# The absolute value of E's phases on VectorE instead of ScalarE, one step ahead, in the last three batches of an S4D kernel

## The chip, the cores and the metric

One core of one Trainium2 chip runs the program alone. The metric is the device time of one execution in microseconds. The kernel before has a median of 719.2 us over three runs (718.16, 719.2 and 723.35). The profile shows one more execution of it, which took 723.32 us.

## What is computed

A block of two branches over 2048 tokens of 448 channels, both residual and behind a layer norm that is scaled and shifted by a modulation of a condition c. The first branch is an S4D state-space convolution, the second a mixer MLP over the tokens (W2 gelu(W1 LayerNorm(h)^T)):

```python
def _A_ref(u, log_A_real, A_imag, C_real, C_imag, log_dt, D_skip):
    L = u.shape[1]
    dt = jnp.exp(log_dt)
    A = -jnp.exp(log_A_real) + 1j * A_imag
    C = (C_real + 1j * C_imag) * dt[:, None]
    P = jnp.exp((A * dt[:, None])[:, :, None] * pos[None, None, :])
    K = 2.0 * jnp.einsum("dn,dnl->dl", C, P).real
    y = jnp.fft.irfft(Uf * Kf[None, :, :], L2)[:, :, :L]
    return y + u * D_skip[None, None, :]
...
h = _layernorm(x, axis=-1) * (1 + ca) + sa
x = x + ga * _A_ref(h, ...)
h = _layernorm(x, axis=-1) * (1 + cb) + sb
x = x + gb * _B_ref(h, ...)
```

Uf and Kf are the rfft of u and K. The part that matters here is K: for each of 448 channels, a sum over 256 states of a complex exponential over 2048 positions. The kernel splits a position into 64 x 32 and writes K as a product of two factors for each channel, E (over 64) and G (over 32), each a magnitude times the cosine and the sine of a phase.

## The kernel before

The channels are taken 16 at a time; a group of 16 has two halves of 128 states, and each half is one *step*: 56 steps, in 7 *batches* of 8. TensorE, ScalarE, VectorE and GpSimd take their instructions in the order in which the program is written; only the DMA queue on SyncE (SP) is ordered by the framework after the first steps.

A batch begins with a *window* (`window(s)`): for each of its 8 steps TensorE makes the exponents (`st_exponents`, L601) and ScalarE takes their Exp (L612) into `mag`. Then ScalarE loads the table of Sin and the 8 steps follow. In a step `s`:

- TensorE makes the phases of step s+1 (`st_phase`, L601): xe (for E) and xg (for G), each one PSUM bank, as four pairs of matmuls, xe and xg in turn. Each name has two buffers, so the phase of step s+1 takes the buffers of step s-1.
- From step 33 on TensorE then makes K of step s-1 (`st_kgen`, L676: 64 small matmuls of E and G into kg).
- ScalarE takes Abs of xe (L642, into `ab`) and of xg (L643), then the Sin of xe in place (L644), of xg (L645), of |xg| (L646) and of |xe| (L647). The last two are cosines: sin(pi/2 - 2 pi |x|). L647 writes into xg.
- GpSimd makes G (L649, L650), VectorE the two sine halves of E (L651, L652), then what `between()` holds, then the two cosine halves of E (L654, L655).
- Behind the step, ScalarE flushes its list: the copy of a finished kg (L690), copies of `vv` (L802), of `y` (L720).

From step 33 on, every second step also carries a *piece* of the convolution: TensorE multiplies a spectrum of K by a table (`pc_s2`, L770, into kx), VectorE multiplies it by the spectrum of u (L779, zx and zy, in the `between()` of the next step), GpSimd combines them (L781, L782, z), TensorE transforms back (`pc_inv`, L796, vv). In the window VectorE also copies `y` out of PSUM (L720). VectorE adds the skip to ks (L695) in the other steps' `between()`.

Behind the batches come the remaining pieces and then the MLP, which TensorE bounds.

Of the kernel before, what the change touches and what calls it, by code (L numbers as in the profile page):

```python
# [10 lines left out]

F32 = mybir.dt.float32
F32R = mybir.dt.float32r
BF16 = mybir.dt.bfloat16
AF = mybir.ActivationFunctionType
ALU = mybir.AluOpType
# [6 lines left out]
P = 128  # L23
# [7 lines left out]
BATCH = 8  # L31
# [129 lines left out]
class WeightStream:  # L161
# [12 lines left out]
    def load(self):  # L174
        n = self.loaded
        if n == 64:
            return
        w = self.pool.tile([P, 896], F32, tag="w", name="w", bufs=3)
        if n < 32:
# [14 lines left out]
    def begin(self, most):  # L194
# [4 lines left out]
        w = self.raw.pop(n)  # L199
        hi = self.pool.tile([P, 896], F32R, tag="whi", name="whi")  # L200
        lo = self.pool.tile([P, 896], F32R, tag="wlo", name="wlo")
        self.nc.scalar.copy(hi, w)  # L202
# [4 lines left out]
    def rest(self, part, eng, load=True):  # L207

        if part:
            w, hi, lo = part  # L210
            eng.tensor_tensor(lo, w, hi.bitcast(F32), ALU.subtract)  # L211
            if load:
# [4 lines left out]
def tile_adaln_s4d_mixer(ctx, tc, i, out):  # L217
# [4 lines left out]
    dram = ctx.enter_context(tc.tile_pool(name="dram", bufs=1, space=DRAM))  # L222
    pars = [dram.tile([2, 3, P, 2, N], F32, name=f"pars{q}") for q in range(4)]
    yu_d = dram.tile([2, 32, 2, 8, 4, D], F32, name="yu_d")
    us_d = dram.tile([2, 32, P, DC], F32, name="us_d")
    v_d = dram.tile([32, P, D], F32, name="v_d")
    x2_d = dram.tile([L, D], F32, name="x2_d")
# [10 lines left out]
    with ExitStack() as es:  # L238
        V, S, G, T = nc.vector, nc.scalar, nc.gpsimd, nc.tensor
        tt, ts, stt = V.tensor_tensor, V.tensor_scalar, V.scalar_tensor_tensor  # L240
# [9 lines left out]
        cg, mp, wp = right("cg", 1), right("mp", 8), right("wp", 2)  # L250
# [15 lines left out]
        def par_load(q):  # L266
            n = min(P, D - P * q)
            raws[q] = {}
            for nm in ("A_C_real", "A_C_imag", "A_log_A_real", "A_A_imag"):
                raws[q][nm] = qp.tile([P, N], F32, tag=nm, name=nm, bufs=2)  # L270
                nc.sync.dma_start(raws[q][nm][0:n], i[nm][P * q : P * q + n])
# [4 lines left out]
        par_load(0)  # L276
        tab = cg.tile([P, 3, 512], F32R, name="tab")
        for v in (2, 1, 0):
# [24 lines left out]

        lph = [cg.tile([P, N], F32R, name=f"lph{k}") for k in range(3)]
        lex = [cg.tile([P, N], F32R, name=f"lex{k}") for k in range(4)]
        for t in lex + lph:
# [56 lines left out]
        def chain(q):  # L363
# [8 lines left out]
            def split(src, places):  # L372
                hl = qp.tile([P, 2, N], F32R, tag="hl", name="hl", bufs=3)[0:n]
                V.tensor_copy(hl[:, 0], src)
                yield
                tt(hl[:, 1], src, hl[:, 0].bitcast(F32), ALU.subtract)
                for k, v in places:
                    nc.sync.dma_start(pars[q][v, k, 0:n], hl.bitcast(F32))
                yield
# [79 lines left out]
        def angle():  # L459

            for a, s, u, xa, ya in tmp.values():
                S.activation(xa, ya, AF.Arctan)
# [25 lines left out]
        nm = xp.tile([P, 16], F32, name="nm")  # L488
# [87 lines left out]
        mags, m2s, eg, phs = {}, {}, {}, {}  # L576
# [20 lines left out]
        def halves(out, lhs, rhs, start, stop):  # L597

            for k in range(2):
                r = slice(64 * k, 64 * k + 64)  # L600
                T.matmul(out[k], lhs[r], rhs[r], start=start, stop=stop)  # L601

        def st_exponents(s):
            g, h = divmod(s, 2)
            phs[s] = [pph.tile([P, 512], F32, tag=nm, name=nm) for nm in ("xe", "xg")]
            halves(phs[s], lex[g % 4][:, h * P : (h + 1) * P], tab[:, 2], True, True)
# [7 lines left out]
        def st_phase(s):  # L614

            g, h = divmod(s, 2)
            lhs = lph[g % 3][:, h * P : (h + 1) * P]
            pm = [pph.tile([P, 512], F32, tag=nm, name=nm) for nm in ("xe", "xg")]
            halves(pm, lhs, tab[:, 1], True, False)
            halves(pm, mg[:, 0], ones, False, False)  # L620
            halves(pm, mg[:, 1], ones, False, False)
            halves(pm, lhs, tab[:, 0], False, True)
            phs[s] = pm

        def st_mag2(s):
# [4 lines left out]
            G.tensor_tensor(m2, me, w[:, :, None].to_broadcast([P, GD, 32]), ALU.mult)  # L630
            m2s[s] = m2

        def st_step(s, between):
            me, mg_, m2 = v32(mags[s][:, 0]), v32(mags[s][:, 1]), m2s.pop(s)
            E = gp_.tile([P, 2, GD, NJ], F32, tag="E", name="E")
            Gt = gp_.tile([P, 2, GD, NI], F32, tag="G", name="G")


            xe, xg = phs.pop(s)
            ab, sg, cg_ = (wp.tile([P, 512], F32, tag=nm, name=nm, bufs=b) for nm, b in (("ab", 1), ("gs", 3), ("gs", 3)))  # L640

            S.activation(ab, xe, AF.Abs)  # L642
            S.activation(cg_, xg, AF.Abs)  # L643
            S.activation(xe, xe, AF.Sin, scale=TWO_PI)  # L644
            S.activation(sg, xg, AF.Sin, scale=-TWO_PI)  # L645
            S.activation(cg_, cg_, AF.Sin, scale=-TWO_PI, bias=math.pi / 2)  # L646
            S.activation(xg, ab, AF.Sin, scale=-TWO_PI, bias=math.pi / 2)  # L647
            se, ce = v32(xe), v32(xg)
            G.tensor_tensor(Gt[:, 1], mg_, v32(sg), ALU.mult)  # L649
            G.tensor_tensor(Gt[:, 0], mg_, v32(cg_), ALU.mult)  # L650
            V.tensor_tensor(E[:, 1, :, 32:64], m2, se, ALU.mult)  # L651
            V.scalar_tensor_tensor(E[:, 1, :, 31::-1], me[:, :, 31::-1], -1.0, se, ALU.mult, ALU.mult)  # L652
            between()
            V.tensor_tensor(E[:, 0, :, 31::-1], me[:, :, 31::-1], ce, ALU.mult)  # L654
            V.tensor_tensor(E[:, 0, :, 32:64], m2, ce, ALU.mult)  # L655
            eg[s] = (E, Gt)
            mags.pop(s)
# [5 lines left out]
        def mellow():  # L663
            ready.extend(fresh)
            fresh.clear()
# [302 lines left out]
        def window(s):  # L968
            angle()
            logs(s == 8)  # L970
            if s == 8:
                u_scale()
                u_norm(0)
                u_norm(1)

            if s in (8, 16):
                for k in (0,) if s == 8 else (4, 5):
                    modulation(k, 0, 1)
            if s == 0:
                st_exponents(s)  # L980
            for e in range(BATCH):
                st_exp(s + e)

                if e + 1 < BATCH:
                    st_exponents(s + e + 1)
                else:
                    st_phase(s)
                mellow()
                if s == 8 and e == 0:
                    tt(mod[1], mod[1], mod[2], ALU.mult)  # L990
                flush(dve)
                flush(act)
                if s < 32:
                    more(WPACE[s // 8][e])
                if s == 0 and e >= 4:
                    u_stats(e - 4)
                if s == 8 and e == 1:

                    tt(mod[0], mod[0], mod[2], ALU.mult)
                if s and e < (2 if s <= 32 else 1):  # L1000
                    st_kgen(s - (2 if s <= 32 else 1) + e)
                elif e == 5:
                    if s == 8:
                        yks[0] = y0.tile([P, 32, DC], F32, tag="yk", name="yk0")
                    st_s1(s > 16)

                if s in (8, 16):
                    some(u_rows, rows, (2, 2, 2, 2, 2, 0, 1, 1)[e])
                elif s == 24 and e != 5:
                    some(u_cols, cols, 1)  # L1010

                if s >= 40 and e == 2:
                    piece(False)
                if s >= 32 and e in (4, 7):
                    piece(e == 4 and pieces[0] < NP, V)
                if s == 0 and e in (4, 5):
                    st_mag2(e - 4)
                elif s and (e < 2 or s >= 32):
                    st_mag2(s + e)
                if s == 8 and e == 0:  # L1020
                    u_norm(e + 2)
                if s == 0 and e == 3:
                    for r in range(4):
                        dsk_copy(r)
            if s == 0:

                S.activation(one, one, AF.Sin)
# [6 lines left out]
        for s in range(tail):  # L1034
            if s == 32:
                early.close()
                fp = es.enter_context(tc.tile_pool(name="fp", bufs=2, reuse_waits="tile"))
# [20 lines left out]
            def between():  # L1058
                flush(dve)
                if 2 <= s < BATCH:  # L1060
                    for r in range(2 * s, 2 * s + 2):
                        u_stats(r)
                if s < len(pace):
                    more(pace[s])
# [110 lines left out]
    with ExitStack() as es:  # L1175
        es.enter_context(tc.manual_schedule(engines={ENG.PE, ENG.Activation, ENG.DVE, ENG.Pool}))
        V, S, G = nc.vector, nc.scalar, nc.gpsimd
# [184 lines left out]
```

## Time and profile before

| | us |
|---|---|
| median of three runs | 719.2 |
| the profiled execution | 723.32 |
| its span, first to last instruction | 721.5 |
| steps 32 to 55 with their windows, from the table load of Exp at 245.41 to the start of the last L655 at 375.52 | 130.1 |
| ScalarE busy over the span | 442.9 |
| VectorE busy over the span | 453.3 |
| TensorE busy over the span | 630.4 |

A row of a timeline has the start in us from the span's start, the duration, the engine, the line, the operation, what it writes and reads, and, in brackets, how long the engine was idle before it and what ended that. Instructions of one engine overlap a little at their ends, so that the time one takes from its engine is read from start to start. A row of the windows view has the stretch and its length, then the busy time of each engine, the granted clock of TensorE, the share of the DMA engines and their rate.

### The profile page before, as it was taken

To read this page: it belongs to the slowest core of one execution; us is meant where nothing else is said; L and a number is where in the kernel's file an instruction comes from. 1 tells how busy PE (TensorE), PEld (TensorE's weight loads), DVE (VectorE), ACT (ScalarE), POOL (GpSimd) and SP (SyncE) were. 2 spreads that over 40 slices of the span, in tenths; PEclk is the share of its full clock that TensorE was granted. 3 is DMA by queue.
4 is the path that set the end of the run, shared out by engine and by line. 5 is a ranking of instruction groups with operands and counts; after the bars stand their busy time and mean duration, and the time that the engine had idled before them with its cause. 6 is when DMAs were issued, how large, how long until landed. Compare 5 with 4: busy or idle time off the path is not lost. (4 is left out here: it accounts for less than half of the span.)

```text
span 721.5 us, 18291 instructions
## 1 busy us (share of the span) xinstructions
PE 630.4 (87%) x7204; PEld 455.2 (63%) x7204; DVE 453.3 (63%) x875; ACT 442.9 (61%) x879; POOL 273.4 (38%) x328
## 2 busy tenths in 40 slices
PE   0659989987899888789888949999999999999997
PEld 0334334543544546556565617778999999999996
DVE  7569779769859768476785538778723263334441
ACT  5837588777988889989983549787622242222220
POOL 6487428318729788878884600000000000000000
PEclk9869857787999999989999959999999999999999
DMA  7795464356889645535236979974585436655540
GB/s 168 203 192 139 147 198 138 114 186 164 245 250 254 183 137 131 162 86 152 71 105 184 289 221 257 243 207 112 167 233 153 143 106 176 175 156 153 154 141 25
DMA packets 101636, 121.19 MB, mean 168 GB/s; under 512 B 13067, under 2 KB 87423, under 8 KB 101423
## 3 DMA queue, kind: packets, MB, share of 16 engines
q1 hardware_dynamic: 100014, 113.16, 55.3%
q0 software_dynamic: 1536, 6.87, 4.4%
q8 instruction: 57, 0.93, 0.6%
q14 instruction: 29, 0.23, 0.1%
HBM read 84.64 MB, written 34.87 MB: 166 GB/s over the span
## 5 line engine op out<-in xcount | busy, mean ns | idle before, releaser
L202 ACT CAST whi<-w 128x896 fp32r<-128x896 f32 x64 | 59.7, 938 | 131.4 <-PE o L1329 84.6
L649 POOL TENSOR_TENSOR G<-mag,gs 128x512 f32<-128x512 f32 x56 | 71.9, 1283 | 92.4 <-ACT gs L645 92.4
L211 DVE TENSOR_TENSOR wlo<-w,whi 128x896 fp32r<-128x896 f32 x64 | 68.0, 1087 | 40.3 <-ACT whi L202 27.9
L601 PE MATMUL xg<-tab,lph 64*128 64x512 f32 x112 | 68.0, 609 | 26.6 <-issue 7.9
L1194 PE MATMUL acc<-h3h,whi 128*128 128x448 f32 x224 | 83.5, 373 | 0.1
L1195 PE MATMUL acc<-h3l,whi 128*128 128x448 f32 x224 | 82.0, 366 | 0.0
L1329 PE MATMUL o<-ul,whi 128*128 128x448 f32 x224 | 81.3, 363 | 0.0
L676 PEld LDWEIGHTS kg<-E,G 128*32 128x32 f32 x3584 | 60.7, 121 | 32.5 <-issue 19.4
L1328 PE MATMUL o<-uh,whi 128*128 128x448 f32 x224 | 81.2, 362 | 0.0
L1196 PE MATMUL acc<-h3h,wlo 128*128 128x448 f32 x224 | 81.1, 362 | 0.0
L1330 PE MATMUL o<-uh,wlo 128*128 128x448 f32 x224 | 80.6, 360 | 0.0
L601 PE MATMUL xe<-tab,lph 64*128 64x512 f32 x112 | 66.7, 599 | 12.2 <-ACT gs L646 10.0
L676 PE MATMUL kg<-E,G 128*32 128x64 f32 x3584 | 70.8, 237 | 3.1 <-issue 2.3
L650 POOL TENSOR_TENSOR G<-mag,gs 128x512 f32<-128x512 f32 x56 | 71.7, 1280 | 0.0
L651 DVE TENSOR_TENSOR E<-m,xe 128x512 f32<-128x512 f32 x56 | 38.2, 683 | 39.6 <-ACT xe L644 31.5
L630 POOL TENSOR_TENSOR m<-mag,w 128x512 f32<-128x512 f32 x56 | 59.9, 1069 | 6.0 <-DVE E L655 1.5
L1332 DVE SCALAR_TENSOR_TENSOR y<-o,b,mod 128x448 f32<-128x448 f32 x16 | 10.9, 684 | 80.3 <-PE o L1330 80.3
L642 ACT ACTIVATE ab<-xe 128x512 f32<-128x512 f32 x56 | 33.6, 600 | 31.0 <-PE xe L601 18.4
L1194 PEld LDWEIGHTS acc<-h3h,whi 128*128 128x128 f32 x224 | 42.4, 189 | 13.9 <-ACT h L1250 6.3
L601 PE MATMUL xe<-tab,lex 64*128 64x512 f32 x56 | 31.2, 567 | 19.2 <-DMA lex<-wm 17.4
L601 PEld LDWEIGHTS xg<-tab,lph 64*128 64x128 f32 x112 | 24.0, 214 | 37.1 <-issue 9.8
L612 ACT ACTIVATE mag<-xe 128x512 f32<-128x512 f32 x56 | 35.5, 634 | 17.8 <-PE xg L601 11.1
(231 smaller groups left out, 1485.9 us busy)
## 6 DMA issues: line engine op xcount, KB each, us to landing
w<-in_B_w_dram SPq DMA_DIRECT2D x64, 224.0 KB
w<-in_B_w_dram SPq DMA_DIRECT2D x32, 448.0 KB
yu_d<-yt SPq DMA_DIRECT2D x16, 448.0 KB
yi<-yu_d SPq DMA_DIRECT2D x32, 224.0 KB
us_d<-uo SPq DMA_DIRECT2D x16, 448.0 KB
u<-us_d SPq DMA_DIRECT2D x32, 224.0 KB
v_d<-vt SPq DMA_DIRECT2D x32, 224.0 KB
vt<-v_d SPq DMA_DIRECT2D x16, 448.0 KB
```

What stands on the lines that cost most here:

```text
L211: eng.tensor_tensor(lo, w, hi.bitcast(F32), ALU.subtract)
L601: T.matmul(out[k], lhs[r], rhs[r], start=start, stop=stop)
L630: G.tensor_tensor(m2, me, w[:, :, None].to_broadcast([P, GD, 32]), ALU.mult)
L649: G.tensor_tensor(Gt[:, 1], mg_, v32(sg), ALU.mult)
L650: G.tensor_tensor(Gt[:, 0], mg_, v32(cg_), ALU.mult)
L676: T.matmul(kgs[g][32 * q : 32 * q + 32, m], Gt[:, c, d], E[:, c, d], start=h == 0 and c == 0 and m == 0, stop=h == 1 and c == 1, skip_grou ...
L1194: nc.tensor.matmul(acc[f], hi[:, fs], h3h[:, r], start=r == 0, stop=False)
L1195: nc.tensor.matmul(acc[f], hi[:, fs], h3l[:, r], start=False, stop=False)
L1196: nc.tensor.matmul(acc[f], lo[:, fs], h3h[:, r], start=False, stop=r == 15)
L1328: nc.tensor.matmul(o, hi[:, ks], uh[kh][:, k], start=kh == 0 and k == 0, stop=False)
L1329: nc.tensor.matmul(o, hi[:, ks], ul[kh][:, k], start=False, stop=False)
L1330: nc.tensor.matmul(o, lo[:, ks], uh[kh][:, k], start=False, stop=kh == 1 and k == 6)
```

## The change

From step 32 on ScalarE no longer makes `ab`. VectorE makes it by clearing the sign bit of xe, read out of PSUM as integers: of step s+1 in step s, behind the two sine products and ahead of `between()` and the two cosine products; of a batch's first step at the end of its window, behind the copies of y. Two buffers of `ab` take turns, one in each of two pools. The steps before 32 are unchanged.

```diff
+        abss = {}
+
+        def st_abs(s, xe):
+            abss[s] = (wp if s < 32 or s % 2 else fp).tile([P, 512], F32, tag="ab", name="ab", bufs=1)
+            if s < 32:
+                S.activation(abss[s], xe, AF.Abs)
+            else:
+                ts(abss[s].bitcast(I32), xe.bitcast(I32), 0x7FFFFFFF, None, ALU.bitwise_and)
+
...
-            ab, sg, cg_ = (wp.tile([P, 512], F32, tag=nm, name=nm, bufs=b) for nm, b in (("ab", 1), ("gs", 3), ("gs", 3)))
-
-            S.activation(ab, xe, AF.Abs)
+            sg, cg_ = (wp.tile([P, 512], F32, tag="gs", name="gs", bufs=3) for _ in range(2))
+
+            if s < 32:
+                st_abs(s, xe)
+            ab = abss.pop(s)
             S.activation(cg_, xg, AF.Abs)
             S.activation(xe, xe, AF.Sin, scale=TWO_PI)
...
             V.scalar_tensor_tensor(E[:, 1, :, 31::-1], me[:, :, 31::-1], -1.0, se, ALU.mult, ALU.mult)
+            if s >= 32 and (s + 1) % BATCH:
+                st_abs(s + 1, phs[s + 1][0])
             between()
...
                     st_phase(s)
+                    if s >= 32:
+                        st_abs(s, phs[s][0])
                 mellow()
```

On VectorE, step 46 (its E is E_5018) and its place before; xe_4896 is the xe of step 46, xe_4975 that of step 47:

```order
L651 TENSOR_TENSOR E_5018<-m2_4542,xe_4896 128x16x32
L652 SCALAR_TENSOR_TENSOR E_5018<-mag_4531,xe_4896 128x16x32
L779 TENSOR_TENSOR zx_5033<-kx_4961,u_4465 128x448
L779 TENSOR_TENSOR zy_5034<-kx_4961,u_4465 128x448
L654 TENSOR_TENSOR E_5018<-mag_4531,xg_4897 128x16x32
L655 TENSOR_TENSOR E_5018<-m2_4542,xg_4897 128x16x32
```

The same step on VectorE now (its E is E_5020, its xe is xe_4898, that of step 47 xe_4977; 14 to 16 lines further down in the file):

```order
L663 TENSOR_TENSOR E_5020<-m2_4542,xe_4898 128x16x32
L664 SCALAR_TENSOR_TENSOR E_5020<-mag_4531,xe_4898 128x16x32
L641 TENSOR_SCALAR ab_5033<-xe_4977 128x512
L793 TENSOR_TENSOR zx_5035<-kx_4963,u_4465 128x448
L793 TENSOR_TENSOR zy_5036<-kx_4963,u_4465 128x448
L668 TENSOR_TENSOR E_5020<-mag_4531,xg_4899 128x16x32
L669 TENSOR_TENSOR E_5020<-m2_4542,xg_4899 128x16x32
```

One instruction has come in, which reads the xe of the next step, and four of this step stand behind it.

On ScalarE, the first step of the batch that begins with step 48, before, with the engines each instruction waits for:

```order
L642 ACTIVATE ab_5376<-xe_5344 128x512 [waits PE_49,Activation_49]
L643 ACTIVATE gs_5378<-xg_5345 128x512 [waits PE_49]
L644 ACT_TABLE_LOAD
L644 ACTIVATE xe_5344<-xe_5344 128x512 [waits Activation_49]
L645 ACTIVATE gs_5377<-xg_5345 128x512
```

The same place on ScalarE now:

```order
L613 ACTIVATE mag_5341<-xg_5332 128x512 [waits PE_49]
L655 ACTIVATE gs_5379<-xg_5345 128x512 [waits PE_49]
L656 ACT_TABLE_LOAD [waits DVE_49]
L656 ACTIVATE xe_5344<-xe_5344 128x512 [waits Activation_49]
L657 ACTIVATE gs_5378<-xg_5345 128x512
```

The Abs is gone, and the table load ahead of the Sin that overwrites xe now waits for VectorE. On VectorE the and of this step stands directly behind the two copies of y:

```order
L734 COPY yk1_3527<-y1_5290 128x32x2x8
L734 COPY yk1_3527<-y1_5291 128x32x2x8
L641 TENSOR_SCALAR ab_5354<-xe_5344 128x512
L663 TENSOR_TENSOR E_5376<-m2_5208,xe_5344 128x16x32
L664 SCALAR_TENSOR_TENSOR E_5376<-mag_5156,xe_5344 128x16x32
```

Before, L651 of this step followed the copies; the and is new there too.

More of the change, by code (lines that the diff above doesn't have):

```diff
@@ L12 @@
 F32 = mybir.dt.float32
+I32 = mybir.dt.int32
 F32R = mybir.dt.float32r
```

## The prediction

> **What bounds the kernel now.** I read the stretch that the change touches, steps 32 to 55, first by its busy times, then engine by engine. Steady steps of the middle batch (40 to 47), as the windows view has them:
>
> ```profile
> core 0: us, PE busy (x) PEld busy (x) DVE busy (x) ACT busy (x) POOL busy (x), PEclk, DMA share, GB/s
> 317.00:333.00 16.00, 13.81 (x382) 9.70 (x380) 14.36 (x26) 15.20 (x33) 13.83 (x14) 1.00 0.45 132
> ```
>
> ScalarE (ACT) is busy 15.20 of 16 us, but VectorE (DVE), TensorE (PE) and GpSimd (POOL) are all near 14. Whoever takes work off ACT has about one microsecond in ten to give. ACT's timeline, from the copy of kg at the end of step 44 to the Sin of step 47:
>
> ```profile
> 321.26 0.37 ACT L690 COPY ks<-kg 128x256 f32<-128x256 f32 x1 [0.32 <-PE kg L676]
> 321.53 0.60 ACT L642 ACTIVATE ab<-xe 128x512 f32<-128x512 f32 x1
> 322.02 0.60 ACT L643 ACTIVATE gs<-xg 128x512 f32<-128x512 f32 x1
> 322.50 0.62 ACT L644 ACTIVATE xe<-xe 128x512 f32<-128x512 f32 x1
> ...
> 329.93 0.62 ACT L644 ACTIVATE xe<-xe 128x512 f32<-128x512 f32 x1
> ```
>
> Instructions overlap at their ends, so I count from start to start: the removed activation is worth 0.49 us (321.53 to 322.02), not its 0.60. Two steps, Sin to Sin, take 7.43 us (322.50 to 329.93). VectorE over the same two steps:
>
> ```profile
> 321.87 0.68 DVE L655 TENSOR_TENSOR E<-m,xg 128x512 f32<-128x512 f32 x1
> 323.22 0.69 DVE L651 TENSOR_TENSOR E<-m,xe 128x512 f32<-128x512 f32 x1 [0.68 <-ACT xe L644]
> 323.82 0.68 DVE L652 SCALAR_TENSOR_TENSOR E<-mag,xe 128x512 f32<-128x512 f32 x1
> 324.42 0.59 DVE L695 TENSOR_TENSOR ks<-ks,dsk 128x4 f32<-128x4 f32 x1
> 324.94 0.67 DVE L654 TENSOR_TENSOR E<-mag,xg 128x512 f32<-128x512 f32 x1
> 325.53 0.68 DVE L655 TENSOR_TENSOR E<-m,xg 128x512 f32<-128x512 f32 x1
> 326.33 0.69 DVE L651 TENSOR_TENSOR E<-m,xe 128x512 f32<-128x512 f32 x1
> 326.93 0.68 DVE L652 SCALAR_TENSOR_TENSOR E<-mag,xe 128x512 f32<-128x512 f32 x1
> 327.53 0.62 DVE L779 TENSOR_TENSOR zx<-kx,u 128x448 f32<-128x448 f32 x1
> 328.07 0.61 DVE L779 TENSOR_TENSOR zy<-kx,u 128x448 f32<-128x448 f32 x1
> 328.60 0.67 DVE L654 TENSOR_TENSOR E<-mag,xg 128x512 f32<-128x512 f32 x1
> 329.19 0.68 DVE L655 TENSOR_TENSOR E<-m,xg 128x512 f32<-128x512 f32 x1
> ```
>
> From L655 of step 44 (321.87) to L655 of step 46 (329.19) is 7.32 us. Without the waits ahead of the two L651, and with 0.60 for each L655 in front of them (as L651 to L652), the slots sum to 0.60+0.60+0.60+0.52+0.59+0.60+0.60+0.60+0.54+0.53+0.59 = 6.37 us. VectorE has 0.95 us free in two steps. In the same stretch TensorE runs, in its own order:
>
> ```profile
> 322.65 0.46 PE L601 MATMUL xg<-tab,lph 64*128 64x512 f32 x1 [1.02 <-ACT gs L643]
> 323.72 1.10 PE L676 MATMUL kg<-E,G 128*32 128x64 f32 x64
> 324.75 0.98 PE L770 MATMUL kx<-yk,si 128*64 128x224 f32 x8
> 325.66 1.03 PE L796 MATMUL vv<-z,si 64*128 64x224 f32 x8
> 326.36 0.56 PE L601 MATMUL xe<-tab,lph 64*128 64x512 f32 x1
> 327.02 0.58 PE L601 MATMUL xe<-tab,lph 64*128 64x512 f32 x1
> ```
>
> The first row is the phase of step 46. Its xg takes the buffer of step 44, so it cannot start before L655 of step 44 has read it: 0.78 us from 321.87 to 322.65 (the row names L643, but L655 ended at 322.55 too). The last two rows are the phase of step 47, which comes behind kgen (L676), L770 and L796; its xe is ready at 327.02 + 0.58 = 327.60.
>
> The delay of a batch reaches the end of the program, since the chain of waits leaves the batches through the last piece without slack:
>
> ```profile
> 379.89 0.08 DVE ks L695
> ...
> 380.06 0.67 POOL z L781
> ...
> 380.77 1.32 PE vv L796 x8
> ```
>
> **What is taken away.** ACT loses 24 activations of 0.49 us, 11.8 us. In each steady pair ACT would need 7.43 - 0.98 = 6.45 us. So another limit comes next.
>
> **What is added on VectorE.** 24 bitwise ands, 128x512, out of PSUM. The nearest row is the copy out of PSUM of the same size; the other two are the slowest and a quick tensor_scalar of half the size, from SBUF:
>
> ```profile
> L720 DVE COPY yk<-y 128x512 f32<-128x512 f32 x14 | 8.9, 678 | 0.9 <-PE y L714 0.9
> L388 DVE TENSOR_SCALAR s<-s 128x256 f32<-128x256 f32 x2 | 1.6, 800 | 0.0
> L423 DVE TENSOR_SCALAR u<-u 128x256 f32<-128x256 f32 x2 | 0.6, 294 | 0.1
> ```
>
> I take 0.60 us from start to start, what L651 to L652 takes at the same 0.68 duration. The ends, from the half sizes, are 2 x 0.29 = 0.59 and 2 x 0.80 = 1.6. Two ands make 1.20 in a pair where 0.95 is free: VectorE alone would need 6.37 + 1.20 = 7.57 us.
>
> **What is moved.** On SP, in several places of these steps, the load of a piece's u now stands behind two loads of lph instead of ahead of them. Each u is loaded three pieces before its zx, each lph two groups before its phase, so I cost this at nothing; without that cover it would be one issue on SP. The order on PE and POOL is as it was.
>
> **The new wait.** The and of step 47 stands in step 46 behind L652 and ahead of zx, zy, L654 and L655. It needs the xe of step 47, and VectorE takes instructions in order. So L654 and L655 of step 46 now wait for TensorE, and L655 is what lets the next phase start. That closes a round through rows above: L655 of step 44 to its released phase 0.78; to kgen 1.07 (322.65 to 323.72); to L770 1.03; to L796 0.91; to the phase of step 47 0.70; to its xe 1.24; a signal 0.06 (estimate); the and 0.60; zx 0.54; zy 0.53; L654 0.59; L655 again. The sum is 8.05 us, against 7.32 before in this round and 7.43 Sin to Sin. Before, only ACT read the xe that was ready at 327.60, and its Sin of it came at 329.93. Behind the waiting and are queued zx and zy (POOL's z waits for them) and the two cosine products (kgen and the next phase wait). A batch has two such rounds (steps 43 to 45 and 45 to 47): +0.73 at VectorE's 7.32, +0.62 at 7.43, together +1.35.
>
> **The start of a batch.** The Sin overwrites xe in place, so the table load ahead of it now waits for the and, which stands behind VectorE's two yk copies. Batch 48:
>
> ```profile
> 343.31 1.27 DVE L720 COPY yk<-y 128x512 f32<-128x512 f32 x2
> ...
> 344.25 0.62 ACT L643 ACTIVATE gs<-xg 128x512 f32<-128x512 f32 x1
> 344.89 1.28 ACT L644 ACT_TABLE_LOAD   x1
> ```
>
> The copies end at 344.58, the and at about 345.2: the load starts 0.3 us later instead of 0.5 earlier. With another and, 0.6, ahead of L654 of the batch's first step, L655 there is about 0.7 later (0.3 + 0.6, less what L654 waited for its cosine, an estimate), and the phase two steps on waits for it; two steps on, ACT waits for kgen:
>
> ```profile
> 305.81 0.76 PE L601 MATMUL xg<-tab,lph 64*128 64x512 f32 x1 [0.98 <-DVE E L655]
> 313.94 0.37 ACT L690 COPY ks<-kg 128x256 f32<-128x256 f32 x1 [2.92 <-PE kg L676]
> ```
>
> Against these 0.7 stands the 0.5 saved behind that copy, and a phase that ran at half clock and would run a little later, at the full one. I take 0, bounds -0.5 and +0.7.
>
> **Sum.** 3 batches x 1.35 = +4.0 us; with the bounds of the start +2.5 to +6.1. The profiled execution took 723.32 us (span 721.5), so it would take 727.3. It is the slow end of the three runs (718.16 to 723.35); on the median of 719.2 the same 4.0 gives **723.2 us**, +0.6%, below the 1% (7.2 us) that a measurement here can tell from no change.
>
> **Rivals.**
>
> *The clock falls within the steps (slower).* TensorE's longest gap in a round is 1.02 now; with rounds of 8 us and no more work it grows to about 1.7 (1.02 + 0.73). The granted clock moves in steps of 3.4 us:
>
> ```profile
> 243.84:247.26 3.42, 2.39 (x68) 1.57 (x68) 3.42 (x7) 3.39 (x7) 2.52 (x2) 0.99 0.39 93
> 247.26:250.67 3.41, 3.41 (x103) 2.80 (x106) 0.72 (x2) 2.23 (x6) 2.58 (x5) 0.51 0.76 228
> ...
> 257.50:260.91 3.41, 1.95 (x17) 1.18 (x16) 1.30 (x3) 3.38 (x6) 2.10 (x4) 1.00 0.35 111
> 260.91:264.32 3.41, 1.59 (x12) 0.79 (x16) 2.48 (x5) 3.41 (x9) 2.45 (x2) 0.99 0.57 179
> ```
>
> It fell to 0.51 behind a stretch with 2.39 us busy, and held behind one with 1.95. A round would leave some 1.7 busy in its emptiest stretch, so either can happen. It decides where a fall meets the 5.0 us of TensorE's links in the round (1.07+1.03+0.91+0.70+1.24): half clock for 3.4 us adds up to 1.7. One fall in each of six rounds is +10.2: 733.4 us. Chance 0.20.
>
> The Trainium skill ("TensorE: Matmul & The Clock Gate", Part 1) says that the clock is halved after an idle window of about 3.4 us and restored after a busy one. By that rule a gap of 1.7 us would cost nothing and the sum would stay 723.2; the trace agrees on the window's length, but its 2.39 us busy ahead of a fall speak against so clean a condition, so I keep the chance.
>
> *VectorE alone bounds.* If the xe is there in time, the rounds take 7.57: +0.25 and +0.14, three times, +1.2: 720.4 us. For it: the wait in my sum is only 0.48 a round. Against: the six rows of TensorE stand in that order whatever VectorE does. Chance 0.21.
>
> *ACT's time is simply won.* 11.8 us off: 707.4. It needs an and below 0.47 us and no wait in VectorE's queue; the L720 row speaks against it. Chance 0.05.
>
> *The and is dear.* At 1.6 us a round grows by another 1.0 and the start of a batch by 1.0: about +4.4 a batch, +13, 732.2 us. For it only the L388 row, which reads SBUF. Chance 0.06.
>
> **How the numbers follow.** My case has 0.48. Its own range is 2.5 to 6.1 on the median, 721.7 to 725.3, and the runs lie 1.0 below to 4.2 above their median. The range 717.5 to 731.0 takes in this, the second rival with that spread, and a clock that falls in about half of the rounds; it leaves out the rest of the clock's, the won ACT and the dear and, some 0.2. Faster by over 1%: only the won ACT, 0.05. Slower by over 1% (above 726.4): most of the clock's 0.20 and the dear 0.06, 0.23. Within: 0.72.
>
> **What would show it.** The and's row near 0.68 us; VectorE waiting for PE's xe ahead of the and in steps 44 and 46; Sin to Sin of 8.0 in the pairs 43 to 45 and 45 to 47; ACT waiting for kg longer than 0.3 to 0.4; the table load of Sin waiting for VectorE. The prediction is wrong if the pairs come out below 7.4, if the and takes half or twice 0.68, or if the clock's row shows 0.5 in steps 43 to 47.

## The result, and the profile after

The changed kernel took **730.2 us** (median of 4 runs, 729.43 to 730.55) against 719.65 (4 runs, 718.16 to 723.35): the ratio is 1.013, 95% interval 1.0097 to 1.0163, so slower, though by less than 2%. On another chip, beside the last experiments, it was 730.63 against 718.74, ratio 1.0179 (1.0155 to 1.0203). The time lies in the predicted range, near its upper end; the likeliest case, 723.2, was 7 us too low.

The profiled execution took 730.55 us. The page's span and the first line of its busy times:

```profile
span 728.8 us, 18271 instructions
PE 631.8 (87%) x7204; PEld 457.2 (63%) x7204; DVE 467.4 (64%) x899; ACT 431.9 (59%) x855; POOL 273.0 (37%) x328
```

ScalarE lost 11.0 us (442.9 before), VectorE gained 14.1, and the span grew by 7.3. The and itself, in the view that groups steps 32 to 55 by line, and what VectorE waited for ahead of it:

```profile
L641 DVE TENSOR_SCALAR ab<-xe 128x512 int32<-128x512 int32 x24 | 16.5, 686 | 10.5 <-PE xg L602 6.2 <-PE xe L602 4.2
L709 DVE TENSOR_TENSOR ks<-ks,dsk 128x4 f32<-128x4 f32 x11 | 7.4, 674 | 4.1 <-ACT ks L704 4.1
```

The and takes 686 ns, and VectorE stood 10.5 us ahead of it until TensorE had made an xe or xg. (Both halves of a phase are made together, so the name of either stands for it.) The second row, the add of the skip to ks, averaged 548 ns over the same eleven adds before; it will matter.

Of these 10.5 us, 4.6 stand in the three rounds in which the clock will be seen to fall, and 5.8 in the first steps of the batches. In the other three rounds the wait is hardly there. VectorE in step 54, one of them:

```profile
378.82 0.67 DVE L664 SCALAR_TENSOR_TENSOR E<-mag,xe 128x512 f32<-128x512 f32 x1
379.53 0.69 DVE L641 TENSOR_SCALAR ab<-xe 128x512 int32<-128x512 int32 x1
```

From start to start this is 0.71 us where 0.60 is the length without a wait; the others are 0.59 to 0.70. What filled the time is told with the experiments.

The Sin of step s to that of step s+2 is one pair. In batch 48, ScalarE's Sin of steps 51, 53 and 55:

```profile
363.73 0.60 ACT L656 ACTIVATE xe<-xe 128x512 f32<-128x512 f32 x1
...
373.31 0.60 ACT L656 ACTIVATE xe<-xe 128x512 f32<-128x512 f32 x1
...
381.44 0.60 ACT L656 ACTIVATE xe<-xe 128x512 f32<-128x512 f32 x1
```

9.58 and 8.13 us. All pairs, read in this way from both profiles (us; the second, fourth, sixth and eighth step of each batch):

| pair of steps | before, batches 32, 40, 48 | after |
|---|---|---|
| 2nd to 4th | 8.16, 9.43, 8.11 | 8.50, 9.59, 8.45 |
| 4th to 6th | 7.33, 7.32, 7.33 | 9.59, 8.19, 9.58 |
| 6th to 8th | 7.43, 7.43, 7.43 | 8.14, 9.44, 8.13 |

Of the six rounds of which the prediction spoke (the last two lines), three take 8.13 to 8.19 and three 9.44 to 9.59. The windows view of the changed kernel, cut at the steps of the clock, shows what the three long ones share:

```profile
core 0: us, PE busy (x) PEld busy (x) DVE busy (x) ACT busy (x) POOL busy (x), PEclk, DMA share, GB/s
270.72:274.13 3.41, 1.79 (x30) 0.96 (x34) 3.41 (x10) 3.03 (x7) 2.60 (x4) 1.00 0.38 103
274.13:277.55 3.42, 3.42 (x67) 2.33 (x58) 3.42 (x6) 2.54 (x5) 2.95 (x3) 0.50 0.65 11
325.33:328.75 3.42, 1.96 (x40) 1.12 (x44) 3.42 (x7) 3.17 (x7) 2.69 (x4) 1.00 0.58 180
328.75:332.16 3.41, 3.41 (x60) 2.29 (x50) 3.41 (x6) 2.31 (x5) 3.12 (x3) 0.50 0.04 14
362.88:366.29 3.41, 1.79 (x31) 0.96 (x30) 3.41 (x7) 2.98 (x7) 2.49 (x4) 1.00 0.25 68
366.29:369.71 3.42, 3.42 (x70) 2.32 (x61) 3.42 (x6) 2.51 (x5) 3.11 (x4) 0.50 0.02 5
```

In each batch, a stretch in which TensorE is busy 1.79 to 1.96 of 3.41 us is followed by one at half clock, in which it is busy throughout. Before, no round held such a stretch.

The ledger of steps 32 to 55 (table load of Exp to the start of the last cosine product): 130.1 before, 245.04 to 384.45 = 139.4 after, +9.3. The three undisturbed rounds give the price of a round at full clock: 4th to 6th 8.19 - 7.33 = +0.86, 6th to 8th 8.135 - 7.43 = +0.70, together +1.56 a batch, +4.7. The clock adds 1.40, 1.39 and 1.30, +4.1. The pairs 2nd to 4th add 0.84, and the part ahead of them gives back 0.3.

### The profile page after: what moved, and what is told of

Same layout as the page of the kernel before. It is cut to its first block, busy times and chain, and to the rows that moved or that the text cites. A ratio compares the mean times of both kernels' runs of the same rounds, so it can differ in the third digit from the quotient of the medians.

```text
span 728.8 us, 18271 instructions
## 1 busy us (share of the span) xinstructions
PE 631.8 (87%) x7204; PEld 457.2 (63%) x7204; DVE 467.4 (64%) x899; ACT 431.9 (59%) x855; POOL 273.0 (37%) x328
## 5 line engine op out<-in xcount | busy, mean ns | idle before, releaser
L690 PE MATMUL kg<-E,G 128*32 128x64 f32 x3584 | 72.3, 240 | 2.8 <-issue 1.3
L1344 PEld LDWEIGHTS o<-uh,whi 128*128 128x128 f32 x224 | 42.0, 188 | 3.4
```

The costliest lines, as they stand in the source:

```text
L690: T.matmul(kgs[g][32 * q : 32 * q + 32, m], Gt[:, c, d], E[:, c, d], start=h == 0 and c == 0 and m == 0, stop=h == 1 and c == 1, skip_grou ...
L1344: nc.tensor.matmul(o, hi[:, ks], uh[kh][:, k], start=kh == 0 and k == 0, stop=False)
```

## The experiments

Times differ by some 9 us in places that no experiment touches: the table load of Exp of step 32, ahead of which all the kernels are alike, starts at 237.2 to 246.2 us in the profiles. So the pairs tell the theories apart, and the ratio only as far as it goes. "Stretch" is the ledger's stretch, and "half clock" says in how many of the six rounds the clock fell.

| run | undisturbed rounds, 4th to 6th and 6th to 8th | half clock | stretch | ratio to before, 95% interval |
|---|---|---|---|---|
| before | 7.33, 7.43 | 0 | 130.1 | |
| after | 8.19, 8.14 | 3 | 139.4 | 1.013 (1.0097 to 1.0163) |
| after_again | 8.14 to 8.20, 8.08 | 2 | 141.5 | 1.0179 (1.0155 to 1.0203) |
| e1_nowait | 8.07, 8.07 | 2 | 136.7 | 1.0046 (1.0011 to 1.0082) |
| e2_warm | 8.11 to 8.20, 8.07 | 0 | 134.3 | 1.0027 (0.9981 to 1.0072) |
| e2_again | 8.12 to 8.18, 8.08 | 0 | 136.8 | 1.0071 (1.0039 to 1.0103) |
| e3_even | 8.55, 8.55 | 1 | 137.5 | 1.0101 (1.0043 to 1.016) |
| e4_first | 8.14 to 8.21, 8.09 | 1 | 136.5 | 1.0094 (1.0061 to 1.0126) |
| e5_pool | 8.04, 8.04 | 2 | 141.0 | 1.0152 (1.0104 to 1.0201) |
| e6_both | 6.91, 7.81 | 1 | 131.4 | 1.0024 (0.9984 to 1.0065) |
| e7_even_pool | 7.41, 7.41 | 0 | 130.0 | 1.0008 (0.9967 to 1.0049) |
| e8_before_pool | 7.07, 7.68 | 0 | 132.9 | 1.0041 (1.0009 to 1.0074) |
| e9_before_warm | 7.33, 7.43 | 0 | 130.1 | 1.001 (0.9984 to 1.0035) |
| e10_even_warm | 7.40, 7.41 | 0 | 131.4 | 0.9996 (0.9963 to 1.0029) |

**e1_nowait: the wait for xe taken away.**

```diff
-                st_abs(s + 1, phs[s + 1][0])
+                st_abs(s + 1, xe)
```

> The and stands at its place in VectorE's queue, but reads the xe of its own step, which VectorE has just read, so that it waits for nothing; of all steps from 32 on but the first of each batch, the absolute value of E's phases is left out. Theory (the wait for the next step's xe closes a round through TensorE, and the longer round lets the clock fall): the pairs 43 to 45 and 45 to 47 take 7.4 to 7.6 us, no half clock in them in any batch, and the time is about 721 us (0.5 of VectorE's slots still added in six rounds, +1.2 on before). Rival (the ands' 1.2 us of VectorE in a pair, or their reading PSUM, is what costs): the pairs stay at 8.1 us or more and the time at 729 to 731.

The wait is gone, and the undisturbed rounds are still 8.07; the clock fell in two others. The median, 721.74, is what the theory said, but not for its reason: the pairs refute it, and in the profile the batches began 6 us sooner than in the changed kernel (239.0 for 245.0). Why its ten runs (718.9 to 727.2) all lie below the nine of the changed kernel (729.4 to 732.4) is not shown by the pairs and stays open. VectorE in steps 51 to 54 of this kernel, grouped by line, has no idle time at all:

```profile
L641 DVE TENSOR_SCALAR ab<-xe 128x512 int32<-128x512 int32 x4 | 2.7, 680 | 0.0
...
L709 DVE TENSOR_TENSOR ks<-ks,dsk 128x4 f32<-128x4 f32 x2 | 2.3, 1170 | 0.0
...
L793 DVE TENSOR_TENSOR zx<-kx,u 128x448 f32<-128x448 f32 x2 | 1.2, 608 | 0.0
```

So VectorE's queue is full at 8.07, not at the 7.57 of the prediction. The difference is the add to ks: 1170 ns for 512 numbers. (From its start to the next it held VectorE for 1.16 and 1.02 us; with the second, 7.57 - 0.52 + 1.02 = 8.07; with the first, 8.21.) In the changed kernel, VectorE and then GpSimd in batch 48:

```profile
375.55 0.68 DVE L641 TENSOR_SCALAR ab<-xe 128x512 int32<-128x512 int32 x1
376.15 0.95 DVE L709 TENSOR_TENSOR ks<-ks,dsk 128x4 f32<-128x4 f32 x1
377.02 0.67 DVE L668 TENSOR_TENSOR E<-mag,xg 128x512 f32<-128x512 f32 x1
```

```profile
375.80 1.28 POOL L662 TENSOR_TENSOR G<-mag,gs 128x512 f32<-128x512 f32 x1
```

The add ends at 377.10, GpSimd's product at 377.08. The same holds at 284.90 and 284.88, 321.81 and 321.78, 367.57 and 367.55. It also held before: the add that took 0.59 there from 324.42 ends at 325.01, and GpSimd's L649 of 1.29 from 323.70 at 324.99. The add waits for the product that GpSimd is making; the and, by coming in ahead of it, moved it from the second half of one product to the early part of the next. The Trainium skill ("SBUF — State Buffer", SBUF: two separate sides) says that a VectorE operation with two inputs from SBUF and a GpSimd operation that reads SBUF exclude each other for the whole instruction. The trace agrees: the add has both inputs in SBUF, while every other VectorE operation of these steps reads one from PSUM and keeps its 0.6 to 0.7 us.

**e5_pool and e6_both: the add to ks on GpSimd,** in the changed kernel and in e1_nowait.

```diff
-                    tt(k0, k0, dsk[:, g, :, None], ALU.add)
+                    (G if g >= 16 else V).tensor_tensor(k0, k0, dsk[:, g, :, None], ALU.add)
```

> Changed kernel with the add of the skip to ks (128x4) on GpSimd instead of VectorE from step 32 on. On VectorE it took 0.87 to 1.16 us of the queue, since it seems to wait for GpSimd's running product G to end. Theory (two limits stand at the same length: the round through TensorE and the xe, which does not hold this add, and VectorE's full queue, which does): only the second gets shorter, so the undisturbed pairs 43 to 45 and 45 to 47 stay at 8.0 to 8.2 us and VectorE gets idle time ahead of the and; 728 to 731. Rival (VectorE's queue alone is the limit): the pairs fall to 7.1 to 7.5 and the time to about 723.

> Both taken away: the and reads the xe of its own step and waits for nothing (the absolute value of all steps from 32 on but the first of a batch is left out), and the add to ks is on GpSimd. Theory (two limits): now the undisturbed pairs fall below those of before, to 7.0 to 7.4 us (VectorE 7.57 - 0.52 = 7.05), and the time to 716 to 719. Rival (a third limit, TensorE's order with the copy of kg on ScalarE, holds the pairs): 7.7 to 8.1, 721 to 724.

With e1 they make a square of the two suspects:

| rounds at full clock | add to ks on VectorE | add to ks on GpSimd |
|---|---|---|
| and waits for the next xe | 8.19, 8.14 | 8.04, 8.04 |
| and waits for nothing | 8.07, 8.07 | 6.91, 7.81 |

Either cure alone brings 0.15 at most; both together bring 1.28 in the first round and 0.33 in the second. Two limits of nearly the same length stood side by side, as the theory had it. With the add on GpSimd, VectorE has idle time again, and it stands where the prediction said, ahead of the and (here the e5_pool kernel in batch 48):

```profile
369.68 0.69 DVE L641 TENSOR_SCALAR ab<-xe 128x512 int32<-128x512 int32 x1 [0.91 <-PE xe L602]
```

On GpSimd the add takes 0.22 us:

```profile
367.25 0.22 POOL L709 TENSOR_TENSOR ks<-ks,dsk 128x4 f32<-128x4 f32 x1
```

The 6th to 8th step of e6_both stays at 7.81, above the 7.0 to 7.4 expected: a third limit, as the rival had it. The median, 721.99, lies in the rival's 721 to 724 too, not in the theory's 716 to 719. ScalarE's timeline shows it waiting for kg ahead of the last Sin of the batch:

```profile
330.13 0.37 ACT L704 COPY ks<-kg 128x256 f32<-128x256 f32 x1 [1.38 <-PE kg L690]
```

**e2_warm and e2_again: TensorE kept busy in the gap.**

```diff
+            if s >= 32 and s % BATCH in (4, 6):
+                for _ in range(3):
+                    T.matmul(pm[0], lhs[0:64], tab[0:64, 1], start=True, stop=True)
             halves(pm, lhs, tab[:, 1], True, False)
```

> Changed kernel, and ahead of the phase of each batch's fifth and seventh step TensorE makes the first matmul of xe three times more into the same place (overwritten by the real one), 1.2 us at full clock in a gap of 1.5 to 1.6. Theory (half of the six rounds are longer by 1.3 to 1.4 because the clock falls behind their gap): the half-clock stretches inside the steps (one in each batch) are gone, all six rounds take 8.1 to 8.3, and the time falls by 3 x 1.4 = 4.1, to about 726. Rival (the fall does not come from the gap, or TensorE's order is the limit): the falls stay and the extra matmuls lengthen the rounds, 730 to 735.

> The kernel of e2_warm once more. If the extra matmuls in the gap keep the clock up: no half clock in the six rounds, all at 8.0 to 8.2 us, and 0.5 to 0.8% (four us and more) below the changed kernel. If its first profile was chance: two to four rounds of 9.3 or more, as in the changed kernel, and the same time.

> The changed kernel once more, beside the next three on one chip. If the falls of the clock inside the steps belong to it: half-clock stretches again in two to four of its six rounds (43 to 45 and 45 to 47 of each batch), 9.3 to 9.6 us there and 8.0 to 8.2 in the others, and 1.0 to 1.5% over the kernel before. If the first profile was chance: none or one, and below 1.0%.

In two profiles no round of twelve saw half clock; of the changed kernel's twelve, five did (its second ratio, 1.0179, is above the 1.0 to 1.5% expected). At full clock the rounds are those of the changed kernel, 8.07 to 8.20. The windows of e2_again in batch 48, through both rounds:

```profile
359.92:363.33 3.41, 2.50 (x73) 1.52 (x72) 3.41 (x7) 3.08 (x7) 3.19 (x4) 1.00 0.25 67
363.33:366.74 3.41, 3.41 (x64) 2.46 (x56) 3.41 (x6) 2.40 (x6) 3.10 (x3) 1.00 0.28 75
366.74:370.16 3.42, 2.65 (x63) 1.75 (x51) 3.42 (x7) 2.66 (x6) 1.99 (x3) 1.00 0.64 198
370.16:373.57 3.41, 3.41 (x86) 2.53 (x84) 3.41 (x6) 2.99 (x7) 3.14 (x4) 1.00 0.07 13
```

The emptiest holds 2.50 us of matmuls instead of 1.79, and the clock stays at 1.00. Work that nobody needs made the kernel faster: on one chip 724.07 us against 730.63. The stretch shrank by 4.7 of these 6.6. Of the 4.7, the six rounds give 2.8, and 1.8 lie in the pairs 2nd to 4th (9.49, 9.92, 9.24 against 9.43, 8.97, 8.48), at which the extra matmuls were not aimed. So a part of the gain is not explained.

**e3_even and e7_even_pool: the and for steps 2, 4 and 6 of a batch only,** the others on ScalarE; e7 with the add to ks on GpSimd as well.

```diff
+        on_act = lambda s: s < 32 or s % BATCH not in (2, 4, 6)
...
-            if s < 32:
+            if on_act(s):
                 S.activation(abss[s], xe, AF.Abs)
...
-            if s >= 32 and (s + 1) % BATCH:
+            if not on_act(s + 1):
                 st_abs(s + 1, phs[s + 1][0])
```

> The and only for steps 2, 4 and 6 of a batch; ScalarE makes the absolute value of the others, as before. The and of an even step stands in the odd step ahead of it, where the xe has long been made. Theory (only the ands of odd steps wait for TensorE): no wait for xe ahead of the and in steps 43 and 45, the pairs take 7.0 to 7.35 us (VectorE 6.37 + 0.60, ScalarE 7.43 - 0.49, the round of before 7.32), no half clock in them, and the time is 717.5 to 719.5. Rival (any and ahead of the cosine products delays L655 and with it kgen and the next phase): pairs of 7.9 to 8.0, 722 to 724.

> The and only for steps 2, 4 and 6 of a batch, as in the run e3_even, and the add to ks on GpSimd. Theory (the pairs of 8.55 in e3_even come from the round L665 - and - add to ks - L671 - phase - kgen - copy of kg - Sin - L665, which holds the add at 1.14): 8.55 - 1.14 = 7.4 us a pair, 718 to 720. Rival (the ands ahead of the cosine products alone make it): 8.0 or more, 722 to 727.

e3 failed its theory and its rival: no and waits for an xe in its rounds, and they are longer than in the changed kernel, 8.55. VectorE's and ScalarE's timelines in batch 40:

```profile
327.40 0.68 DVE L643 TENSOR_SCALAR ab<-xe 128x512 int32<-128x512 int32 x1
328.00 1.23 DVE L711 TENSOR_TENSOR ks<-ks,dsk 128x4 f32<-128x4 f32 x1
...
329.74 0.68 DVE L671 TENSOR_TENSOR E<-m,xg 128x512 f32<-128x512 f32 x1
```

```profile
332.80 0.37 ACT L706 COPY ks<-kg 128x256 f32<-128x256 f32 x1 [2.08 <-PE kg L692]
```

Here the and alone pushes the add to the very start of GpSimd's product, 1.23 us, and L671 late; phase, kgen, the copy of kg and the next Sin follow from it, and ScalarE waits 2.08 us. e7 takes the add out of this round: 7.41, as 8.55 - 1.14 foretold, and the time is that of the kernel before.

**e8_before_pool: the add to ks on GpSimd in the kernel before** (the diff of e5).

> The kernel before with nothing changed but the add to ks, which goes to GpSimd from step 32 on. Theory (it stands on VectorE between the sine and the cosine products of every second step, 0.52 us, and the round of before runs through it): the pairs 45 to 47 go from 7.43 to 6.9 to 7.2 us, and the time falls by 1 to 3 us. Rival (ScalarE, busy 15.20 of 16 us, holds the pairs): 7.3 to 7.45, no change.

The first round gained 0.26, the second lost 0.25 (7.68). The pair that the theory named is the one that lost; no gain.

**e4_first: the first step of a batch back on ScalarE** (the diff of e3, with `s % BATCH == 0`).

> Changed kernel, but the absolute value of the first step of each batch is back on ScalarE, so that the table load of the Sin waits for no and. Theory (the start of a batch costs nothing on balance): 729.5 to 731, the pairs as in the changed kernel. Rival (the load that waits for VectorE sets the batch later by some 0.3 to 1 us): 727 to 729.

The undisturbed rounds are those of the changed kernel, and the Sin table load comes 14.06, 11.81 and 11.81 us behind that of Exp, against 13.71, 11.72 and 12.30 in the changed kernel and 14.61, 12.29 and 12.30 in its second profile: the wait for VectorE costs 0.5 in one batch of three by the first, in all three by the second. The median, 727.2, is the rival's (727 to 729), 3.0 to 3.4 below the changed kernel's two; one or two half clocks fewer account for 1.4 to 2.8 of it. The term is small; its exact size stays open.

**e9_before_warm and e10_even_warm: extra matmuls at the start of a batch,** in the kernel before and in e7_even_pool.

```diff
+            for _ in range({1: 5, 2: 3}.get(s % BATCH, 0) if s >= 32 else 0):
+                T.matmul(pm[0], lhs[0:64], tab[0:64, 1], start=True, stop=True)
             halves(pm, lhs, tab[:, 1], True, False)
```

> The kernel before, with five extra matmuls ahead of the phase of each batch's second step and three ahead of that of its third (into xe, overwritten by the real ones), where TensorE has its gaps of 2.3 and 1.0 us at the start of a batch. Theory (a low clock follows these gaps in every batch and lengthens steps 41 to 43): no half clock there, the pair 41 to 43 goes from 8.1 to 9.4 down to 7.3 to 7.8 us, and the time falls by 2 to 5 us. Rival (that pair is held by the order of ScalarE and VectorE, or the clock falls all the same): unchanged, -1 to +1.

> The kernel of e7_even_pool (the and for steps 2, 4 and 6 of a batch, the add to ks on GpSimd) with the same extra matmuls at the start of a batch. Theory: pairs of 7.4 us as there, the pair 41 to 43 at 7.4 to 7.8, and 2 to 5 us below e7_even_pool, 714 to 717. Rival: as e7_even_pool, 718 to 720.

Both rivals held: the pairs 2nd to 4th take 8.12, 9.36 and 8.08 in the first, 8.13, 9.30 and 9.56 in the second. The windows of e9_before_warm at the start of two batches:

```profile
255.08:258.50 3.42, 2.22 (x12) 1.22 (x11) 2.49 (x5) 3.42 (x9) 2.52 (x2) 1.00 0.53 177
258.50:261.91 3.41, 3.41 (x74) 2.47 (x72) 2.85 (x5) 3.38 (x8) 2.52 (x2) 0.50 0.14 46
296.04:299.46 3.42, 1.92 (x12) 1.23 (x10) 1.93 (x4) 3.41 (x8) 2.95 (x5) 1.00 0.37 111
299.46:302.87 3.41, 3.40 (x37) 1.65 (x40) 2.47 (x5) 3.38 (x8) 2.42 (x3) 0.50 0.29 87
```

With the filling TensorE was busy 2.22 and 1.92 us of the stretches ahead, and the clock fell all the same. No version that ran beats the kernel before by more than its interval.

## Why the prediction was right or wrong

- **ScalarE's 11.8 us.** Right: 11.0 less busy, and nothing of it reached the end.
- **The price of the and.** Right: 0.60 from start to start, 686 ns.
- **The round of 8.05.** Right in size: 8.13 to 8.19 at full clock, +1.56 a batch for +1.35. That its path, through TensorE and the waiting and, is a limit of this length is shown by e5 (8.04 with VectorE partly idle). But it was half of the truth, and in part luck: the wait of 0.48 that it held for VectorE came to 0.11 at most in the undisturbed rounds, because the add to ks had filled that time. Its 0.06 for a signal had no row behind it: the and starts 0.03 to 0.04 behind the end of the last matmul of its phase (279.26 to 279.29, 371.45 to 371.49).
- **"VectorE alone would need 7.57".** Wrong: 8.07 (e1). The step took the add to ks at the 0.52 that it filled before. It was a wait for GpSimd whose length depends on when the add comes, and behind the and it held VectorE for 0.76 to 0.97 in the changed kernel and up to 1.16 in e1. The rival built on it, 720.4, did not come, and the square of e1, e5 and e6 shows that removing the wait alone shortens these rounds by 0.12 at most.
- **The clock.** This is the step of the likeliest case that failed. The prediction saw the 1.7 us gap and the stretch with "some 1.7 busy", priced a fall at up to 1.7, and gave it 0.20, outside the likeliest sum. Its own sign of being wrong came true in batch 40: the clock's row shows 0.50 from 328.75. It fell in three of six rounds, at 1.30 to 1.40: 4.1 of the 5.3 us by which the steps exceeded the forecast's 4.0. The other 1.2 are the rounds' 0.2 a batch and the start of the batches. By the rule quoted from the Trainium skill ("TensorE: Matmul & The Clock Gate", Part 1) the gap was to cost nothing; the windows with 1.79 to 1.96 us busy ahead of a fall speak against it, and e2 shows that filling the gap ends the falls. The range held the time because it had been drawn to take in a clock that falls in about half of the rounds; the result slower by over 1% had been given only 0.23.
- **The start of a batch, taken at 0 (-0.5 to +0.7).** +0.84 - 0.3 over three batches, within the bounds; the table load waited for the and 2.2 us in all.
- **SP's order, taken at nothing.** Right: in the steps no zx waited for its u.
- **The medians.** The steps grew by 9.3, the span by 7.3, the medians by 10.5. The profiled execution of before took 723.32, 3.7 above the median, which the prediction knew and carried over as a difference. The 2.0 between the steps and the span stand ahead of the stretch (245.04 against 245.41) and behind it (344.4 against 346.0). What lies behind it takes 343.6 to 347.9 in all the profiles, so this is no effect that can be told from chance.

## What to carry to other kernels

A slot read from a trace is a duration only if the instruction does not wait inside itself: a tiny operation that takes half a microsecond is worth a look at what the neighbouring engine ends at the same moment. When a change adds a wait, price the engine that is made to idle as well: here the gap in TensorE cost nearly as much through its clock as the longer round did. And two limits of nearly the same length hide each other, so that each must be taken away alone and both together before one of them is named.

## What was not expected of the hardware

The clock does not follow the busy time of a window alone. It fell behind 1.79, 1.96 and 2.22 us of 3.41, and held behind 2.50. But in the changed kernel itself it held behind 2.04 and 1.99, in the rounds that stayed at full clock:

```profile
373.12:376.53 3.41, 1.99 (x71) 1.47 (x71) 3.41 (x7) 3.06 (x7) 3.21 (x4) 1.00 0.33 92
376.53:379.95 3.42, 3.42 (x72) 2.48 (x64) 3.38 (x6) 2.45 (x6) 3.04 (x3) 1.00 0.23 65
```

Over the rounds of all fourteen profiles, the twelve falls came behind stretches with 1.79 to 2.02 us busy, and no stretch with more than 2.03 was followed by one; but in e4_first the clock held behind 1.79 (309.97 to 313.39). So a stretch so empty is where a fall can come, and what decides it is not shown. And e2_again, at the start of batch 48, held behind 1.78 and fell only behind the next:

```profile
346.26:349.68 3.42, 1.78 (x14) 1.15 (x14) 1.36 (x3) 2.62 (x5) 2.60 (x5) 1.00 0.28 88
349.68:353.09 3.41, 1.06 (x8) 0.61 (x8) 3.41 (x7) 3.41 (x9) 2.77 (x3) 1.00 0.25 85
353.09:356.50 3.41, 3.41 (x73) 2.45 (x71) 3.35 (x6) 3.01 (x7) 2.92 (x3) 0.50 0.00 0
```

And VectorE's wait for GpSimd stands in the trace as the duration of the waiting instruction, not as idle time ahead of it: 0.83 to 1.24 us for an add of 128x4 that GpSimd makes in 0.22.
